# A two-stage kernel's 8th rows: from the absorb stage to sums over all modes at the end

## The chip, the core and the metric

The kernel runs on one core of a Trainium2 chip. The core has TensorE (PE in the profile; its weight loads are PEld), VectorE (DVE), ScalarE (ACT), GpSimd (POOL) and SyncE (SP), and 16 DMA engines that serve the transfers which SP and GpSimd issue. Each engine works through its own instructions in order. The metric is the device time of one execution in microseconds, as the median of several runs. The profile is of one execution more.

## The reference

Two stages in one kernel. The first is a linear attention over q, k, v of 8 batches, 8 heads, 576 rows and 64 columns; its result x has 8 batches of 576 rows and 512 columns. The second mixes x along the rows in the frequency domain and then along the columns:

```python
X = np.fft.rfft(x, axis=1)                     # 64 modes are kept
Yr = einsum('bmd,mde->bme', Xr, w_r) - einsum('bmd,mde->bme', Xi, w_i)
Yi = einsum('bmd,mde->bme', Xr, w_i) + einsum('bmd,mde->bme', Xi, w_r)
y = np.fft.irfft(Y, n=S, axis=1)               # Y is 0 beyond mode 63
u = x + y
return u + np.maximum(u @ w_ch, 0.0)
```

w_r and w_i are 64 matrices of 512 x 512 in f32, 134 MB together; every one is read once. w_ch is one matrix of 512 x 512.

## The kernel before

**Rows.** x lies in SBUF as bf16 (tile xs), in 36 chunks of 128 rows x 512 columns: (bp, n) with batch pair bp 0 to 3 and n 0 to 8. A batch's 576 rows are 64 groups of nine. Chunks n = 0 to 3 hold two of the first eight rows of the groups of the pair's first batch, n = 4 to 7 those of its second batch; chunk n = 8 holds the ninth row of the groups ("8th", counted from 0), of both batches, 64 partitions each. A matmul for n = 8 is therefore made in two halves of 64 output rows (`back`, line 681).

**Weights.** GpSimd issues the loads of the mode weights, cast to bf16 on the way: 64 tiles `wt` of 1 MB each, one for a quarter g of the columns and a group o of eight modes and the real or imaginary part. A load is issued when a buffer comes free, eight buffers in the pool `pw`. `mix` (line 447) multiplies a tile into the sums of its mode group, so TensorE takes each tile once, in the order of the loads.

**y and z.** When the last quarter of a mode group o is mixed (loop at line 848, g = 3, i = 1), the group's mode values are complete: yst (128 x 512). `put` (line 762) copies it to 16 partitions of 8 x 512, the rows from 16 o of `yall` for o under 6, and for o = 6 and 7 to `yl`, in two places of four (32 rows each). TensorE transposes yst and multiplies it by w_ch; that is zst, put to `zall` or to the other two places of `yl`. For o = 7 one of the two copies of each goes through GpSimd's queue, the other through SP's.

**Sums.** irfft is a matmul with a table of cosines and sines over the mode rows. CI is the table for the modes of o = 0 to 5 (96 rows), and it has rows for all 128; CL is the table for the rows of `yl` (o = 6, 7), CM that for o = 7 straight from yst. Since u @ w_ch = x @ w_ch + irfft(Y) @ w_ch, x and x @ w_ch (tile xw) are treated alike, y serves the one and z the other.

**Work that fills the waits for weights.** `todo` (line 753) is a list of steps, of which the loop takes a number after each mix, written in the line with `left`:

- `hold(i)`, one for each chunk: the chunk is transposed and multiplied by w_ch; ScalarE writes the product to xw. The last three chunks (i from K = 33) keep it in PSUM. It also advances the making of the tables (`inverse_tables`).
- the absorb steps (class Absorb, line 691): `all` adds the sums over the modes of o = 0 to 5 to a chunk: one matmul over `yall` for x, one with the identity for xw and one over `zall`; VectorE writes x back to xs, ScalarE xw. For the three held chunks there is only_x and only_w.

The number taken after each mix is such that A steps are left when seven mixes are left, and these are spread over the seven.

**The end.** `Last` (line 771) makes the output of two chunks (the first two and the last two of the list one by one): `base` puts xw or x into PSUM through a permutation or, for n = 8, the identity; `late` adds the sums over `yl`; `relu` is ScalarE's, from PSUM into the tile rl; `store` is VectorE's addition of PSUM and rl into a tile `of` or `ofr`, and SP's transfer to HBM. `seq` (line 844) is the order, with the pairs of n = 8 between those of the other chunks; the last loop (line 914) interleaves `base` and `late` of one entry with those of the next. PSUM has four single banks for the relu part (tag pt) and two pairs for the other (tag pp). Every instruction is kept in the order in which it is written.

Of the kernel before, what the change touches and what calls it, by code (L numbers as in the profile page):

```python
# [10 lines left out]
F32 = mybir.dt.float32  # L11
BF16 = mybir.dt.bfloat16
# [9 lines left out]
NP = 4  # L22
# [21 lines left out]
def kernel(  # L44
# [531 lines left out]
    yall = pw.tile([128, B_, DMODEL], BF16, name="yall", tag="wt")  # L576
    yl = pw.tile([128, B_, DMODEL], BF16, name="yl", tag="wt")
    CI = pb.tile([128, 5, 128], BF16, name="CI", bufs=1)
    CL = pb.tile([128, 5, 128], BF16, name="CL", bufs=1)
    perm = CF.rearrange("p c t x m -> p (c t x m)")[:, 512:640]  # L580
    dve.tensor_copy(perm.rearrange("k (p a) -> k a p", a=2),
                    ident_b.rearrange("k (a p) -> k a p", a=2))
# [3 lines left out]
    def inverse_tables():  # L586

        flat = xw[:, NP - 1].rearrange("p n e -> p (n e)").bitcast(F32)
        tok, ang, rnd = (flat[:, 640 * i:640 * i + 640] for i in range(3))
        small = pb.tile([128, 40], F32, name="small", bufs=1)  # L590
        ints = pb.tile([128, 16], I32, name="ints", bufs=1)
        for c in range(4):
            for a in range(2):
                dve.tensor_scalar_add(out=tok[:, 128 * c + 64 * a:128 * c + 64 * a + 64],
                                      in0=nine, scalar1=float(4 * a + c))
        for i in range(2):
            dve.tensor_scalar_add(out=tok[:, 512 + 64 * i:576 + 64 * i], in0=nine, scalar1=8.0)
        used = [0, 0]
        yield

        def bits(src, shift, mask):
            t, f = ints[:, used[0]:used[0] + 1], small[:, used[1]:used[1] + 1]
            used[0] += 1
            used[1] += 1
            dve.tensor_scalar(out=t, in0=src, scalar1=shift, scalar2=mask,
                              op0=ALU.logical_shift_right, op1=ALU.bitwise_and)
            dve.tensor_copy(f, t)
            return f

        def calc(in0, s1, s2, op0=ALU.mult, op1=ALU.add):  # L610
            f = small[:, used[1]:used[1] + 1]
            used[1] += 1
            dve.tensor_scalar(out=f, in0=in0, scalar1=s1, scalar2=s2, op0=op0, op1=op1)
            return f

        j, t, r = bits(pi, 2, 3), bits(pi, 1, 1), bits(pi, 0, 1)
        jt = calc(t, 4.0, j)
        mode = calc(bits(pi, 4, 7), 8.0, jt)
        late = calc(calc(bits(pi, 4, 1), 8.0, 48.0), 1.0, jt)
        jm, tm, rm, b0 = bits(pi, 5, 3), bits(pi, 4, 1), bits(pi, 3, 1), bits(pi, 0, 7)  # L620
        last = calc(calc(tm, 4.0, jm), 1.0, 56.0)
        b0 = calc(b0, 0.0, 1.0, ALU.is_equal, ALU.mult)
        yield
        for dst, m, r, only in ((CI, mode, r, None), (CL, late, r, None), (CM, last, rm, b0)):
            n = 512 if only is not None else 640
            ph = calc(r, -S_ / 4.0, S_ / 4.0)
            amp = calc(r, -4.0 / S_, 2.0 / S_)
            if m is mode:
                half = calc(calc(m, 0.0, -0.5, ALU.is_equal, ALU.mult), 1.0, 1.0)
                amp = calc(amp, half, 0.0)  # L630
            if only is not None:
                amp = calc(amp, only, 0.0)
            dve.tensor_scalar(out=ang[:, :n], in0=tok[:, :n], scalar1=m, scalar2=ph,
                              op0=ALU.mult, op1=ALU.add)
            dve.tensor_scalar(out=rnd[:, :n], in0=ang[:, :n], scalar1=1.0 / S_, scalar2=MAGIC,
                              op0=ALU.mult, op1=ALU.add)
            dve.tensor_scalar(out=rnd[:, :n], in0=rnd[:, :n], scalar1=-MAGIC,
                              scalar2=-float(S_), op0=ALU.add, op1=ALU.mult)
            dve.tensor_tensor(out=ang[:, :n], in0=ang[:, :n], in1=rnd[:, :n], op=ALU.add)
            yield  # L640
            act.activation(rnd[:, :n], ang[:, :n], ACT.Sin, scale=2.0 * math.pi / S_)
            if dst is CI:
                dve.tensor_scalar_mul(out=dst.rearrange("p c s -> p (c s)"), in0=rnd[:, :n],
                                      scalar1=amp)
                yield
                continue
            for c in range(4):
                dve.tensor_scalar_mul(
                    out=dst[:, c, :].rearrange("k (p a) -> k a p", a=2),
                    in0=rnd[:, 128 * c:128 * c + 128].rearrange("k (a p) -> k a p", a=2),  # L650
                    scalar1=amp)
            if dst is CL:
                dve.tensor_scalar_mul(out=dst[:, 4, :], in0=rnd[:, 512:640], scalar1=amp)
            yield

    class Channels:
# [73 lines left out]
            self.keep_w()  # L730

    chunks = [(bp, n) for bp in range(NP) for n in range(9)]
    ch = [Channels(*c) for c in chunks]
    ab = [Absorb(*c) for c in chunks]
    K = len(ch) - 3
# [15 lines left out]
        ch[i].hold(ab[i].q)  # L751

    todo = [ch[0].turn] + [lambda i=i: hold(i) for i in range(len(ch))]
    todo += [c.only_x for c in ab[K:]] + [c.only_w for c in ab[K:]] + [c.all for c in ab[:K]]
    A = 3 * 3 + K

    def fill(n):
        for _ in range(n):
            if todo:
                todo.pop(0)()  # L760

    def put(src, o, dst, copies):
        if o < 6:
            sp.dma_start(dst[16 * o:16 * o + 16], src)
        else:
            for s in copies:
                r = 32 * s + 16 * (o - 6)
                (sp, pool)[s // 2 if o == 7 else 0].dma_start(yl[r:r + 16], src)


    class Last:

        def __init__(self, *items):
            self.items = items
            bp, n = items[0]
            self.early = bp == 0 and n < 4
            self.first = bp == 0 and n < 2

        def base(self, which):
            if self.first:  # L780
                if which:
                    self.pp = banks()
                    self.q, self.p = [self.pp[:, 1]], [self.pp[:, 0]]
            elif which:
                self.q = [bank() for _ in self.items]
            else:
                self.pp = banks()
                self.p = [self.pp[:, a] for a in range(2)]
            for a, (bp, n) in enumerate(self.items):
                turned = perm if n < 8 else ident_b  # L790
                if which:
                    pe.matmul(self.q[a], lhsT=turned, rhs=xw[:, bp, n, :],
                              start=True, stop=False)
                else:
                    pe.matmul(self.p[a].rearrange("p (g e) -> p g e", g=4), lhsT=turned,
                              rhs=chunk(bp, n), start=True, stop=False)

        def late(self, which):
            for a, (bp, n) in enumerate(self.items):
                r = 64 * a + 32 * which  # L800
                back((self.q if which else self.p)[a], n, bp, CL, yl,
                     slice(r, r + 16 if self.early else r + 32), not self.early)
# [9 lines left out]
            act.copy(self.rl[:, 0], self.p[0])  # L812

        def relu(self):
            self.rl = pb.tile([128, 2, DMODEL], F32, name="rl")
            for a in range(len(self.items)):
                act.activation(self.rl[:, a], self.q[a], ACT.Relu)

        def store(self):
            (bp, n), w = self.items[0], len(self.items)  # L820
# [8 lines left out]
                dve.tensor_tensor(out=o, in0=self.p[0], in1=self.rl[:, 0], op=ALU.add)  # L829
            else:  # L830
                dve.tensor_tensor(out=o, in0=self.pp, in1=self.rl, op=ALU.add)
            if n == 8:
                sp.dma_start(
                    bass.AP(tensor=out.tensor, offset=out.offset + (2 * bp * S_ + 8) * DMODEL,
                            ap=[[9 * DMODEL, 128], [2 * S_ * DMODEL, 2], [1, DMODEL]]), o)
                return
# [4 lines left out]
                o.rearrange("p a e -> p (a e)") if w > 1 else o)  # L841

    pairs = [[((bp, n), (bp, n + 1)) for n in (0, 2, 4, 6)] for bp in range(NP)]
    seq = [Last((0, 0)), Last((0, 1))] + [Last(*x) for x in pairs[0][1:] + pairs[1]]
    seq += [Last((0, 8), (1, 8))] + [Last(*x) for x in pairs[2]] + [Last((2, 8), (3, 8))]
    seq += [Last(*x) for x in pairs[3][:3]] + [Last((3, 6)), Last((3, 7))]
    H = DMODEL // 2
    while mixq:
        key = mixq.pop(0)
# [13 lines left out]
        if g == NG - 1 and i == 1:  # L863
# [8 lines left out]
            for h in range(2):  # L872
                dve.tensor_tensor(out=yst[:, H * h:H * h + H], in0=py[:, H * h:H * h + H],
                                  in1=yacc[:, o, H * h:H * h + H], op=ALU.add)
            put(yst, o, yall, (0, 2))
            if o < 5:
                fill(min(n, 1))
            for h in range(2):
# [22 lines left out]
            act.copy(zst[:, 0:H], pz[0])  # L901
            dve.tensor_copy(zst[:, H:], pz[1])
            put(zst, o, zall, (1, 3))
            fill(max(n - 2, 0) if o < 5 else n)
        else:
            fill(n)
# [7 lines left out]
    for g, s in enumerate(seq):  # L914
# [12 lines left out]
        if t:  # L927
            t.straight(1)
            t.relu()
        s.store()  # L930
    pb_cm.__exit__(None, None, None)
    pw_cm.__exit__(None, None, None)

# [28 lines left out]
```

## Time and profile before

| | |
|---|---|
| median of 7 runs | 444.36 us (443.9 to 445.51) |
| profiled execution, its own time | 444.95 us |
| its span, first to last instruction | 443.1 us |
| TensorE busy, with weight loads beside it | 343.1 us (77%), 218.6 us (49%) |
| VectorE, ScalarE, GpSimd busy | 284.3 (64%), 279.7 (63%), 84.5 us (19%) |
| DMA moved | 99.31 MB, mean 224 GB/s |
| HBM read, written | 163.64 MB, 9.44 MB |
| chain that ended last, largest shares | issue 32%, PE 26%, DMA 15%, ACT 10% |

The span is cut into 40 slices of 11 us. A digit of a slice is the busy share in tenths. A group of instructions is named by its engine, operation and tiles, `out<-in`, with the shape. Line numbers in the profile are those of a helper (L37) for all, so the tiles tell what an instruction is. Times of an instruction are from the start of the span. A transfer lands when all 16 of its parts have. The chain of waits is followed back from the last instruction, at each step to what released it.

### The profile page before, as it was taken

How to read it: one execution, taken by the hardware profiler on the slowest of the kernel's cores; microseconds unless marked ns; L12 is line 12 of the kernel's file. 1: busy time of each engine (PE TensorE's matmuls, PEld its weight loads, DVE VectorE, ACT ScalarE, POOL GpSimd, SP SyncE). 2: the span in 40 equal slices, each digit the busy share in tenths (PEclk: the TensorE clock that was granted, in tenths of full speed). 3: DMA queues.
4: the chain of work that ended last, by engine and by line, in shares of the span. 5: the costliest groups of instructions: out<-in, count | busy, mean ns of one | idle time of the engine just before them, and what ended most of it. 6: DMA issues, size and time to landing. Idle time of an engine off the chain costs nothing.

```text
span 443.1 us, 10508 instructions
## 1 busy us (share of the span) xinstructions
PE 343.1 (77%) x4433; PEld 218.6 (49%) x4433; DVE 284.3 (64%) x561; ACT 279.7 (63%) x488; POOL 84.5 (19%) x126
## 2 busy tenths in 40 slices
PE   3577669677687685885976877886899779999994
PEld 2355547545465573664754655653455434343231
DVE  4657585555765757867668568658834223776685
ACT  4588697666977967867778659433444222665673
POOL 7132122122211212321232121141012110000000
PEclk9979897689988969988889789698999888999998
DMA  8999999999999999999999999999999999993697
GB/s 168 236 211 210 238 211 237 238 212 264 210 213 237 238 236 235 212 238 211 239 222 227 236 213 238 212 212 212 212 224 221 219 219 219 211 221 69 215 383 286
DMA packets 51487, 99.31 MB, mean 224 GB/s; under 512 B 2480, under 2 KB 13616, under 8 KB 51440
## 3 DMA queue, kind: packets, MB, share of 16 engines
q0 software_dynamic: 45280, 86.19, 99.0%
q1 hardware_dynamic: 6160, 12.45, 8.0%
q8 instruction: 34, 0.56, 0.5%
q14 instruction: 13, 0.11, 0.1%
HBM read 163.64 MB, written 9.44 MB: 391 GB/s over the span
## 4 chain that ended last, share of the span: by engine, by line
issue 32%; PE 26%; DMA 15%; ACT 10%; DVE 8%; POOL 7%; POOLq 0%; ACTq 0%; DVEq 0%
DMA wt<-in_moe_w_i_dram 13%; PE pt L37 8%; PE one L37 7%; PE pp L37 5%; PE two L37 5%; POOL wt L37 4%; ACT AB L37 4%; DVE m L37 3%; DVE mk L37 2%; ACT AQ L37 2%; DMA qb<-in_q_dram 1%; ACT XT L37 1%; POOL kb L37 1%; POOL qb L37 1%; POOL vn L37 1%
## 5 line engine op out<-in xcount | busy, mean ns | idle before, releaser
L37 ACT ACTIVATE AB<-two 128x1024 bf16<-128x1024 f32 x64 | 62.1, 1028 | 12.1 <-DVE mk L37 8.6
L37 ACT ACTIVATE AQ<-two 128x1024 bf16<-128x1024 f32 x64 | 62.7, 1047 | 3.5 <-PE two L37 3.4
L37 ACT CAST xw<-pt 128x512 bf16<-128x512 f32 x50 | 29.4, 587 | 40.5 <-PE pt L37 34.9
L37 DVE TENSOR_REDUCE mk<-two 128x8 f32<-128x1024 f32 x32 | 38.9, 1219 | 14.7 <-PE two L37 14.7
L37 DVE TENSOR_REDUCE m<-two 128x8 f32<-128x1024 f32 x32 | 39.2, 1224 | 12.7 <-PE two L37 12.5
L37 DVE RECIPROCAL rd<-one 128x6 f32<-128x6 f32 x48 | 9.4, 196 | 56.0 <-PE one L37 55.9
L37 PE MATMUL pt<-wchb,xT 128*128 128x512 bf16 x136 | 38.2, 407 | 5.8 <-DVE xT L37 4.7
L37 DVE TENSOR_TENSOR va<-vn,ee 128x1152 bf16<-128x1152 f32 x32 | 42.0, 1355 | 0.0
L37 ACT COPY kT<-one 128x512 bf16<-128x512 bf16 (+1 forms) x32 | 19.3, 640 | 31.0 <-PE one L37 30.8
L37 PEld LDWEIGHTS <-xs 128*128 128x128 bf16 x624 | 32.3, 104 | 12.9 <-issue 7.1
L37 PEld LDWEIGHTS <-minus 96*128 96x128 bf16 x288 | 27.9, 115 | 17.5 <-issue 12.3
L37 PE MATMUL two<-w2blk,qT 128*128 128x256 bf16 x128 | 20.8, 289 | 19.1 <-ACT AB L37 9.2
L37 POOL DMA_DIRECT2D wt<-in_moe_w_r_dram x30 | 22.3, 744 | 69.2 <-PE one L37 34.8
L37 POOL DMA_DIRECT2D wt<-in_moe_w_i_dram x28 | 20.9, 746 | 72.6 <-PE one L37 40.0
L37 PE MATMUL two<-qT,w2blk 128*128 128x512 bf16 x64 | 30.2, 472 | 3.8 <-ACT AQ L37 3.7
L37 PEld LDWEIGHTS <-qT 128*128 128x128 bf16 x144 | 14.3, 102 | 36.7 <-issue 33.9
L37 PE MATMUL one<-wt,XT 128*32 128x512 bf16 x304 | 26.6, 436 | 6.1 <-DVE XT L37 2.7
L37 PE MATMUL two<-mT,minus 96*128 96x128 bf16 x256 | 30.7, 255 | 0.0
L37 PE MATMUL one<-kvz,AQ 128*128 128x65 bf16 x512 | 29.5, 217 | 0.0
L37 DVE TENSOR_TENSOR xs<-one,rd 128x384 bf16<-128x384 f32 x48 | 26.8, 557 | 1.6
L37 PEld LDWEIGHTS <-XT 128*32 128x32 bf16 x512 | 14.4, 149 | 26.1 <-issue 14.5
L37 PE MATMUL two<-w2blk,kT 128*128 128x256 bf16 x128 | 21.2, 294 | 7.9 <-ACT AB L37 7.9
(131 smaller groups left out, 701.0 us busy)
## 6 DMA issues: line engine op xcount, KB each, us to landing
wt<-in_moe_w_r_dram POOLq DMA_DIRECT2D x30, 1024.0 KB, 22.2
wt<-in_moe_w_i_dram POOLq DMA_DIRECT2D x28, 1024.0 KB, 22.0
vn<-in_v_dram POOLq DMA_DIRECT2D x15, 576.0 KB, 17.9
out_dram<-of SPq DMA_DIRECT2D x16, 512.0 KB, 3.1
kb<-in_k_dram POOLq DMA_DIRECT2D x16, 288.0 KB, 15.5
qb<-in_q_dram POOLq DMA_DIRECT2D x16, 288.0 KB, 15.5
xs<-in_moe_w_i_dram POOLq DMA_DIRECT2D x2, 1024.0 KB, 24.5
yacc<-in_moe_w_r_dram POOLq DMA_DIRECT2D x1, 1024.0 KB, 9.5
```

What stands on the lines that cost most here:

```text
L37: ins = f(*args, **kwargs)
```

## The change

The four chunks n = 8 are no longer absorbed. They come first in the list of chunks, and the three chunks that are held in PSUM are now (3,5), (3,6) and (3,7) instead of (3,6), (3,7) and (3,8). At the end their sums run over all 128 rows of `yall` and `zall` with the table CI, in one matmul per half; for this the rows of o = 6 and 7 are put into `yall` and `zall` as well, by one more copy on SP after each put (list `rest`). `base` for x is dropped; GpSimd adds x to the relu's output in place (tile rx, from the pool `pw`), and VectorE adds the sum from PSUM as before. The two entries of n = 8 leave `seq`; their first half is done at the end of the last loop's steps 3 and 9, their second half and store at the end of steps 5 and 11. CL loses its fifth column block.

```diff
--- before.py
+++ after.py
@@ -576,7 +576,8 @@
     yall = pw.tile([128, B_, DMODEL], BF16, name="yall", tag="wt")
     yl = pw.tile([128, B_, DMODEL], BF16, name="yl", tag="wt")
     CI = pb.tile([128, 5, 128], BF16, name="CI", bufs=1)
-    CL = pb.tile([128, 5, 128], BF16, name="CL", bufs=1)
+    CL = pb.tile([128, 4, 128], BF16, name="CL", bufs=1)
+    rest = []
     perm = CF.rearrange("p c t x m -> p (c t x m)")[:, 512:640]
     dve.tensor_copy(perm.rearrange("k (p a) -> k a p", a=2),
                     ident_b.rearrange("k (a p) -> k a p", a=2))
@@ -622,7 +623,7 @@
         b0 = calc(b0, 0.0, 1.0, ALU.is_equal, ALU.mult)
         yield
         for dst, m, r, only in ((CI, mode, r, None), (CL, late, r, None), (CM, last, rm, b0)):
-            n = 512 if only is not None else 640
+            n = 640 if dst is CI else 512
             ph = calc(r, -S_ / 4.0, S_ / 4.0)
             amp = calc(r, -4.0 / S_, 2.0 / S_)
             if m is mode:
@@ -649,8 +650,6 @@
                     out=dst[:, c, :].rearrange("k (p a) -> k a p", a=2),
                     in0=rnd[:, 128 * c:128 * c + 128].rearrange("k (a p) -> k a p", a=2),
                     scalar1=amp)
-            if dst is CL:
-                dve.tensor_scalar_mul(out=dst[:, 4, :], in0=rnd[:, 512:640], scalar1=amp)
             yield
 
     class Channels:
@@ -730,6 +729,7 @@
             self.keep_w()
 
     chunks = [(bp, n) for bp in range(NP) for n in range(9)]
+    chunks.sort(key=lambda c: c[1] < 8)
     ch = [Channels(*c) for c in chunks]
     ab = [Absorb(*c) for c in chunks]
     K = len(ch) - 3
@@ -751,8 +751,8 @@
         ch[i].hold(ab[i].q)
 
     todo = [ch[0].turn] + [lambda i=i: hold(i) for i in range(len(ch))]
-    todo += [c.only_x for c in ab[K:]] + [c.only_w for c in ab[K:]] + [c.all for c in ab[:K]]
-    A = 3 * 3 + K
+    todo += [c.only_x for c in ab[K:]] + [c.only_w for c in ab[K:]] + [c.all for c in ab[NP:K]]
+    A = 3 * 3 + K - NP
 
     def fill(n):
         for _ in range(n):
@@ -763,6 +763,7 @@
         if o < 6:
             sp.dma_start(dst[16 * o:16 * o + 16], src)
         else:
+            rest.append((dst[16 * o:16 * o + 16], src))
             for s in copies:
                 r = 32 * s + 16 * (o - 6)
                 (sp, pool)[s // 2 if o == 7 else 0].dma_start(yl[r:r + 16], src)
@@ -775,6 +776,7 @@
             bp, n = items[0]
             self.early = bp == 0 and n < 4
             self.first = bp == 0 and n < 2
+            self.direct = n == 8
 
         def base(self, which):
             if self.first:
@@ -787,7 +789,9 @@
                 self.pp = banks()
                 self.p = [self.pp[:, a] for a in range(2)]
             for a, (bp, n) in enumerate(self.items):
-                turned = perm if n < 8 else ident_b
+                turned = ident_b if self.direct else perm
+                if self.direct and not which:
+                    continue
                 if which:
                     pe.matmul(self.q[a], lhsT=turned, rhs=xw[:, bp, n, :],
                               start=True, stop=False)
@@ -797,6 +801,10 @@
 
         def late(self, which):
             for a, (bp, n) in enumerate(self.items):
+                if self.direct:
+                    back((self.q if which else self.p)[a], n, bp, CI, zall if which else yall,
+                         slice(0, 128))
+                    continue
                 r = 64 * a + 32 * which
                 back((self.q if which else self.p)[a], n, bp, CL, yl,
                      slice(r, r + 16 if self.early else r + 32), not self.early)
@@ -812,9 +820,16 @@
             act.copy(self.rl[:, 0], self.p[0])
 
         def relu(self):
-            self.rl = pb.tile([128, 2, DMODEL], F32, name="rl")
+            if self.direct:
+                self.rl = pw.tile([128, 2, DMODEL], F32, name="rx", tag="wt")
+            else:
+                self.rl = pb.tile([128, 2, DMODEL], F32, name="rl")
             for a in range(len(self.items)):
                 act.activation(self.rl[:, a], self.q[a], ACT.Relu)
+            if self.direct:
+                for a, c in enumerate(self.items):
+                    x = self.rl[:, a].rearrange("p (g e) -> p g e", g=4)
+                    pool.tensor_tensor(out=x, in0=x, in1=chunk(*c), op=ALU.add)
 
         def store(self):
             (bp, n), w = self.items[0], len(self.items)
@@ -829,7 +844,7 @@
                 dve.tensor_tensor(out=o, in0=self.p[0], in1=self.rl[:, 0], op=ALU.add)
             else:
                 dve.tensor_tensor(out=o, in0=self.pp, in1=self.rl, op=ALU.add)
-            if n == 8:
+            if self.direct:
                 sp.dma_start(
                     bass.AP(tensor=out.tensor, offset=out.offset + (2 * bp * S_ + 8) * DMODEL,
                             ap=[[9 * DMODEL, 128], [2 * S_ * DMODEL, 2], [1, DMODEL]]), o)
@@ -841,9 +856,9 @@
                 o.rearrange("p a e -> p (a e)") if w > 1 else o)
 
     pairs = [[((bp, n), (bp, n + 1)) for n in (0, 2, 4, 6)] for bp in range(NP)]
-    seq = [Last((0, 0)), Last((0, 1))] + [Last(*x) for x in pairs[0][1:] + pairs[1]]
-    seq += [Last((0, 8), (1, 8))] + [Last(*x) for x in pairs[2]] + [Last((2, 8), (3, 8))]
+    seq = [Last((0, 0)), Last((0, 1))] + [Last(*x) for x in pairs[0][1:] + pairs[1] + pairs[2]]
     seq += [Last(*x) for x in pairs[3][:3]] + [Last((3, 6)), Last((3, 7))]
+    whole = {5: Last((0, 8), (1, 8)), 11: Last((2, 8), (3, 8))}
     H = DMODEL // 2
     while mixq:
         key = mixq.pop(0)
@@ -873,6 +888,8 @@
                 dve.tensor_tensor(out=yst[:, H * h:H * h + H], in0=py[:, H * h:H * h + H],
                                   in1=yacc[:, o, H * h:H * h + H], op=ALU.add)
             put(yst, o, yall, (0, 2))
+            if rest:
+                sp.dma_start(*rest.pop())
             if o < 5:
                 fill(min(n, 1))
             for h in range(2):
@@ -901,6 +918,8 @@
             act.copy(zst[:, 0:H], pz[0])
             dve.tensor_copy(zst[:, H:], pz[1])
             put(zst, o, zall, (1, 3))
+            if rest:
+                sp.dma_start(*rest.pop())
             fill(max(n - 2, 0) if o < 5 else n)
         else:
             fill(n)
@@ -928,6 +947,16 @@
             t.straight(1)
             t.relu()
         s.store()
+        if g + 2 in whole:
+            d = whole[g + 2]
+            d.base(1)
+            d.late(1)
+            d.relu()
+        if g in whole:
+            d = whole[g]
+            d.base(0)
+            d.late(0)
+            d.store()
     pb_cm.__exit__(None, None, None)
     pw_cm.__exit__(None, None, None)
```

## The prediction

> **What bounds the kernel now.** I read the slices of the page, then the chain of waits, then the weight loads one by one, because the change takes TensorE work out of the last 45 us and adds transfers there. The page's DMA line comes first.
>
> ```profile
> DMA  8999999999999999999999999999999999993697
> q0 software_dynamic: 45280, 86.19, 99.0%
> ```
>
> The 16 DMA engines are full in every slice but the last four: the weights are the bound until shortly before the end. The chain of waits (start, length, what) shows the last wait on weights and the end:
>
> ```profile
> 329.47 31.97 DMA wt<-in_moe_w_i_dram
> ...
> 406.26 0.60 PE pt L37 x7
> ...
> 410.43 3.68 DMA yl<-zst
> ...
> 437.37 0.69 DVE ofr L37
> ```
>
> From 361.5 the chain names TensorE (PE) alone, so 4 us less of it looks like 4 us gained. The view by tile of the last load and of the copies at mode group 6, and the timeline of the mixes that take the last loads, say otherwise:
>
> ```profile
> L37 POOL DMA_DIRECT2D wt<-in_moe_w_i_dram x1: 740/740/740, 370.2 to 370.2; - x1
> DMA to landing us min/median/max: 35.2/35.2/35.2
> ```
>
> ```profile
> L37 SPq DMA_DIRECT2D yl<-yst x2: 547/570/592, 386.7 to 387.3; - x2
> L37 SPq DMA_DIRECT2D yl<-zst x2: 547/574/602, 388.8 to 389.4; - x2
> DMA to landing us min/median/max: 6.6/9.4/10.4
> ```
>
> ```profile
> 402.05 0.66 PE L37 MATMUL pt<-wt,XT 128*32 128x512 bf16 x8
> ...
> 406.19 0.67 PE L37 MATMUL pt<-wt,XT 128*32 128x512 bf16 x8
> ```
>
> The last weight lands at 370.2 + 35.2 = 405.4 and its mix starts at 406.19: 0.8 us of slack. Asked the same way, the loads issued at 342.1, 346.5, 351.9, 357.3 and 362.9 took 35.3, 35.9, 35.7, 36.1 and 37.5: they land at 377.4, 382.4, 387.5, 393.4 and 400.4, against mixes at 379.4, 385.1, 392.4, 397.0 and 402.05. TensorE is never far behind the stream. Two stretches of the clock matter too (length, busy time of PE, PEld, DVE, ACT, POOL, clock, DMA share, GB/s):
>
> ```profile
> 357.95:361.36 3.41, 1.32 (x10) 0.65 (x8) 0.42 (x1) 1.17 (x2) 0.10 (x1) 1.00 1.12 216
> 361.36:364.77 3.41, 2.56 (x16) 1.05 (x16) 1.05 (x3) 0.37 (x1) 0.74 (x1) 0.50 1.12 218
> ```
>
> TensorE was busy 39% of one stretch and ran at half clock in the next.
>
> **What the skill says.** "DMA: Bandwidth & Descriptors", on queues, rings and completion order: an engine goes round between the queues that have work, packet by packet. The trace agrees: a copy from SP lands in 3.4 us at 407.7, when nothing else moves, and in 6.6 to 10.4 us at 387, inside the stream; each takes the stream's time. "TensorE: Matmul & The Clock Gate", Part 1: a free-running window of about 3.4 us with little work halves the clock of the next. The stretches above agree. "GPSIMD Engine Reference", section 3.1: a two-input add of 2048 f32 columns takes 4497 ns; no GpSimd add is in this trace. Its section 1 has GpSimd contend with VectorE instructions that have two SBUF inputs; the tail's VectorE adds read one operand from PSUM, so I expect none.
>
> **The change, part by part.**
>
> *Absorb stage, removed.* Four `all` steps go. A step of an 8th row takes 1.00 us of PE (five matmuls, 398.99 to 399.99), another 0.655 (three at 0.218). The three held chunks become (3,5) to (3,7), so the removed ones are three of the first kind and one of the second, and the two half-width pairs of (3,8) (0.33) become single passes (0.22): 3.0 + 0.655 + 0.22 = 3.9 us of PE. VectorE loses four adds of 0.69 and ScalarE four casts of 0.59, both beside PE. By the quotas of the filling rule all four go before the second last mix. The shorter CL table and the other order of the holds lie before 361.5, where PE waited 2.2 us for weights; without that cover they are some tenths.
>
> *Copies, added.* SP issues four more copies of 128 KB, each behind the put of its y or z. Two fall into the stream (group 6). The spacing of landings without copies is 5.0 and 5.1 (377.4, 382.4, 387.5); the next three took 17.9 in place of 15.1 with four copies among them, so 0.7 per copy, and two more cost 1.4: the last load lands at 406.8, the one before at 401.8 (the copies come earlier, since PE is ahead). Bounds: 0, if the slowest DMA engine had other work, and 2 x 1.0. I take 1.4, since all engines share each copy.
>
> *What then bounds the last mix.* PE is at the second last mix at 402.05 - 3.9 = 398.2 and waits until 401.8. A wait of 3.6 us leaves one clock window mostly idle, so the next 3.41 us run at half clock and lose up to 1.7. What lies between the last two mixes takes 4.14 (402.05 to 406.19): PE is ready at 405.9, or 407.6 in the bad case. With the load at 406.8 I take 407.2: **+1.0 us** (from -0.8, copies free, to +1.5). The 3.9 us become idle time.
>
> *Behind the last mix.* The chain y, transposes, z, put, landing (7.96 us to 414.15) stays. The third y copy on SP is out at 408.8, before SP's z put at 409.89. The third z copy (410.45) shares the engines with GpSimd's z put (410.43), which releases the tail at 414.11: eight packets more per engine against it, and so does the first store's in the kernel before; **+0.3** (0 to 0.7). SP's queue then holds the first store, wanted at 411.13 and free to go at 411.0.
>
> *The tail.* A usual step of two rows is 1.30 us of PE (415.75 to 417.05), 1.24 of VectorE and 512 KB, which at 400 GB/s is 1.31: three engines equally full. Each of the two 8th-row items made two steps 1.63 long: 2 x 1.63 - 1.30 = 1.96, together 3.92. Now each item puts 2 base passes (0.44) and two half-width pairs (0.22 each and 0.1 for the switch) in one place, where nothing is stored, and the next base waits about 0.1 for a bank that ScalarE reads late: 1.1 us without a store. Two steps later come two pairs and a store, 0.54 on PE but 1.24 on VectorE, which now sets the pace. VectorE: 2 x (1.1 + 1.24) = 4.7; it regains 0.06 per step over some six steps: 4.35. At 1.31 per store DMA regains less: **+0.6** in all. Bounds: -0.7 (PE alone: 2 x (0.44 + 0.54 + 0.1 + 0.54) - 3.92), +0.9.
>
> GpSimd: 512 / 2048 of 4497 ns is 1.12 us, say 1.2 with its start, two per item, hidden by the two steps until the item's store. By the same step times they may take 1.6 each; beyond that VectorE waits in order, with all later stores behind it: each 0.1 more costs 0.4 (two adds, two items). From below: a free add gains nothing.
>
> *Sum.* 1.0 + 0.3 + 0.6 = 1.9. The profiled execution took 444.95 (its span of 443.1 and 1.85 around it) and would take 446.85; it is 0.59 over the median of the runs, so **446.3 us** for the median, 0.4% slower. I take any difference under 0.2% (0.9 us) as none.
>
> **The rivals.** (1) The stream doesn't mind the copies and PE counts: the last mix starts at 405.45 (-0.75), the put is not disturbed, the tail gains its 0.7 of PE: 442.9, faster; were PE the only bound, 3.9 + 0.7 less, 439.8. For it: the chain of waits names PE. Against: the landing at 405.4. It decides from copies under 0.27 each (2 x 0.27 - 0.75 - 0.7 = -0.9). (2) A draw: copies at 0.35 each with the clock kept up (+0.3 at the mix), +0.1 at the put, +0.3 in the tail: 445.0. (3) GpSimd is late: 2.2 us per add, 0.6 over its cover, 4 x 0.6 = 2.4 more: 448.7. (4) The new copies write rows 96 to 127 of tiles of which absorb reads rows 0 to 95; if the waits went by tile, PE would stand for a copy at group 6 (6.6 to 10.4, partly in its new slack). Against: matmuls read yl at 409.24 while a copy into its next 16 rows is under way. It would add some 4: 450.
>
> **Chances.** Forecast 0.62, (1) 0.12, (2) 0.16, (3) 0.07, (4) 0.03. The forecast's own range is 445.3 to 447.4 (its terms at +0.6, 0, +0.3 and at +1.4, +0.7, +0.9). The range for 8 in 10 leaves out (3), (4) and about half of (1): 443.8 to 447.8. Slower: 0.70 (the forecast, (3), (4), less a little that falls under 0.2%); faster 0.12; the same 0.18.
>
> **What would show it.** Right: PE idle about 3 us before the second last mix, behind a weight; the last weight landing 1 to 1.5 later than 405.4; some 3.4 us at half clock near 403; six SP copies in a row at group 6; in the tail two gaps of about 2.4 between stores, VectorE without gaps after them. Wrong: the last landing at 405.4; no idle PE before 406; VectorE waiting for GpSimd; ten or more us between a copy's issue and the next absorb matmul.

## The result, and the profile after

The changed kernel takes 448.84 us (median of 12 runs, 447.2 to 451.32); the kernel before, on the same chips, 445.04 (31 runs). The ratio is 1.0092, 95% interval 1.0078 to 1.0107: 4.1 us slower, where 1.9 us slower was predicted. (The ratio is over all runs, close to that of the means; the two medians lie 3.8 us apart.) The profiled execution took 451.32 us with a span of 449.5; it is the longest of the twelve, so its losses are on the large side.

The page of the changed kernel, its line of the DMA engines' busy tenths and that of SP's queue, which had 6160 packets and 12.45 MB before:

```profile
DMA  8999999999999999999999999999999999995498
q1 hardware_dynamic: 6736, 12.98, 9.2%
```

The engines are full as long as before; the slices between the stream and the stores have 5 and 4 where they had 3 and 6. The timeline of the last two mixes after (start, length; in brackets the idle time before it and what ended it), and the last load's landing by tile:

```profile
402.06 0.66 PE L37 MATMUL pt<-wt,XT 128*32 128x512 bf16 x8 [2.73 <-DMA wt<-in_moe_w_r_dram]
...
407.56 0.66 PE L37 MATMUL pt<-wt,XT 128*32 128x512 bf16 x8
```

```profile
L37 POOL DMA_DIRECT2D wt<-in_moe_w_i_dram x1: 740/740/740, 370.9 to 370.9; - x1
...
DMA to landing us min/median/max: 35.8/35.8/35.8
```

TensorE's saved work has become a wait of 2.73 us for a weight, and the last mix starts at 407.56 instead of 406.19, 0.9 us behind the landing at 406.7. That 0.9 is the clock: from one mix to the next TensorE took 5.50 us, where it took 4.14 before. The stretches of the clock's grid after (length, busy PE, PEld, DVE, ACT, POOL, clock, DMA share, GB/s):

```profile
399.59:403.00 3.41, 0.94 (x10) 0.42 (x10) 0.39 (x1) 0.90 (x2) 0.00 (x0) 1.00 1.07 179
403.00:406.41 3.41, 3.41 (x10) 1.06 (x7) 1.29 (x2) 1.14 (x2) 0.00 (x0) 0.50 0.42 79
...
413.24:416.65 3.41, 1.89 (x9) 0.49 (x7) 1.52 (x2) 0.96 (x3) 0.00 (x0) 1.00 1.15 116
416.65:420.06 3.41, 2.63 (x9) 0.54 (x8) 0.00 (x0) 0.94 (x2) 0.00 (x0) 0.50 0.81 291
420.06:423.48 3.42, 3.42 (x13) 0.74 (x10) 1.22 (x1) 2.17 (x4) 0.79 (x1) 0.50 0.14 56
```

There are two stretches at half clock. The first, from 403.00, I had predicted. The second lasts 6.8 us, stands at the start of the tail and was in no step of mine. What leads to it is in the chain of waits after, and in the timelines of the first matmuls that read the two z puts, after and then before:

```profile
411.81 5.58 DMA yl<-zst
417.39 0.04 issue
417.43 1.55 PE pt L37 x3
...
443.83 0.69 DVE ofr L37
```

```profile
415.98 0.37 PE L37 MATMUL pt<-yl,CL 32*128 32x512 bf16 x1 [1.22 <-DMA yl<-zst]
...
417.43 0.58 PE L37 MATMUL pt<-yl,CL 32*128 32x512 bf16 x1 [1.08 <-DMA yl<-zst]
```

```profile
414.15 0.37 PE L37 MATMUL pt<-yl,CL 32*128 32x512 bf16 x1 [0.43 <-DMA yl<-zst]
```

GpSimd's put of z, which releases the tail, took 5.58 us from issue to landing in place of 3.68. TensorE stood 1.22 us for SP's put and 1.08 for GpSimd's, where it had stood 0.43. The span's 6.4 us (449.5 - 443.1) fall apart at these marks: last mix 407.56 against 406.19, +1.4; last mix to landing of the z put 9.83 against 7.92, +1.9; landing to the start of the last VectorE addition 26.44 against 23.26, +3.2.

### The profile page after: what moved, and what is told of

Same layout as the page of the kernel before. It is cut to its first block, busy times and chain, and to the rows that moved or that the text cites. A ratio compares the mean times of both kernels' runs of the same rounds, so it can differ in the third digit from the quotient of the medians.

```text
span 449.5 us, 10464 instructions
## 1 busy us (share of the span) xinstructions
PE 344.9 (77%) x4409; PEld 219.5 (49%) x4409; DVE 281.1 (63%) x556; ACT 278.0 (62%) x484; POOL 89.0 (20%) x130
## 5 line engine op out<-in xcount | busy, mean ns | idle before, releaser
L37 ACT CAST xw<-pt 128x512 bf16<-128x512 f32 x48 | 28.2, 587 | 37.6 <-PE pt L37 33.9
L37 PE MATMUL pt<-wchb,xT 128*128 128x512 bf16 x136 | 37.1, 397 | 6.9 <-DVE xT L37 5.6
L37 PE MATMUL one<-kvz,AQ 128*128 128x65 bf16 x512 | 31.1, 223 | 0.0
L37 POOL DMA_DIRECT2D kb<-in_k_dram x16 | 11.5, 718 | 88.8 <-PE one L37 87.2
L37 PEld LDWEIGHTS <-AQ 128*128 128x128 bf16 x512 | 27.9, 119 | 1.6 <-issue 0.4
```

The source lines that it names most:

```text
L37: ins = f(*args, **kwargs)
```

## The experiments

All ratios are to the kernel before, run on the same chip; microseconds are what the ratio makes of 444.9, so they can differ by some tenths from the difference of two medians. "Behind the last mix" means the two copies of mode group 7, "in the stream" those of group 6.

**Each part alone.** First the four copies alone, in the kernel before:

```diff
         else:
+            rest.append((dst[16 * o:16 * o + 16], src))
             for s in copies:
...
             put(yst, o, yall, (0, 2))
+            if rest:
+                sp.dma_start(*rest.pop())
...
             put(zst, o, zall, (1, 3))
+            if rest:
+                sp.dma_start(*rest.pop())
```

> The kernel before with nothing but the four new copies on SP (into rows of yall and zall that nothing reads); all 8th rows are absorbed as before. Theory A (the copies are the cost: two in the weight stream hold the last load back by about 1.3 us, two behind the last mix hold the z put back by about 2 us): the last mix about 0.5 us later than before, the z put's landing about 2 us later, 447.0 to 448.5. Theory B (the tail with its GpSimd adds and gaps is the cost): 445.0 to 445.5.

It took 448.17 us, ratio 1.0078 (1.0057 to 1.0100), +3.5 us. The copies by themselves make nearly the whole loss. The last load landed at 406.3, 44.9 us after the eighth load before it (43.9 before); GpSimd's z put took 5.56.

The 8th rows not absorbed, alone:

```diff
+    chunks.sort(key=lambda c: c[1] < 8)
...
-    todo += [c.only_x for c in ab[K:]] + [c.only_w for c in ab[K:]] + [c.all for c in ab[:K]]
-    A = 3 * 3 + K
+    todo += [c.only_x for c in ab[K:]] + [c.only_w for c in ab[K:]] + [c.all for c in ab[NP:K]]
+    A = 3 * 3 + K - NP
```

> The kernel before with the chunks of the 8th rows put first and not absorbed, nothing else: no new copies, the old tail. It leaves the modes of groups 0 to 5 out of the 8th rows. Theory A: TensorE's 3.9 us become a wait for weights, the last mix starts at 405.4 to 406.2, 444.2 to 445.0. Rival (the new wait before the second last mix halves the clock and costs more than it gives): 445.5 or more.

It took 443.69 us, ratio 0.9987 (0.9977 to 0.9998), -0.6 us. That is half a microsecond under theory A's range, but the kernel before took 444.41 on this chip. 3.9 us of TensorE work are worth 0.6. The timeline of the mixes:

```profile
395.11 0.66 PE L37 MATMUL pt<-wt,XT 128*32 128x512 bf16 x8
400.23 0.66 PE L37 MATMUL pt<-wt,XT 128*32 128x512 bf16 x8 [1.07 <-DMA wt<-in_moe_w_r_dram]
405.24 0.66 PE L37 MATMUL pt<-wt,XT 128*32 128x512 bf16 x8 [0.81 <-DMA wt<-in_moe_w_i_dram]
```

TensorE waits for the last two loads, and its last mix starts 0.04 us after the landing at 405.20.

The changed tail alone; the diff is to the changed kernel:

```diff
-    chunks.sort(key=lambda c: c[1] < 8)
...
-    todo += [c.only_x for c in ab[K:]] + [c.only_w for c in ab[K:]] + [c.all for c in ab[NP:K]]
-    A = 3 * 3 + K - NP
+    todo += [c.only_x for c in ab[K:]] + [c.only_w for c in ab[K:]] + [c.all for c in ab[:K]]
+    A = 3 * 3 + K
...
-            if rest:
-                sp.dma_start(*rest.pop())
...
-            if rest:
-                sp.dma_start(*rest.pop())
...
-                     slice(0, 128))
+                     slice(0, 96))
```

> The changed tail alone: 8th rows absorbed as before, no new copies, the tail of the changed kernel with the sums over 96 rows (so it counts groups 0 to 5 twice for the 8th rows and leaves 6 and 7 out). My term of +0.6 us: 445.3 to 446.0. Theory B (the tail is the cost): 447 or more. GpSimd's two adds 2.3 us per item, hidden.

It took 445.30 us, ratio 1.0015 (1.0003 to 1.0027), +0.7 us. VectorE's and GpSimd's timelines of this kernel:

```profile
419.23 2.52 DVE L37 TENSOR_TENSOR of<-pp,rl 128x1024 f32<-128x1024 f32 x2 [1.14 <-PE pp L37]
421.67 1.21 DVE L37 TENSOR_TENSOR of<-pp,rx 128x1024 f32<-128x1024 f32 x1
422.89 5.11 DVE L37 TENSOR_TENSOR of<-pp,rl 128x1024 f32<-128x1024 f32 x4
```

```profile
418.43 2.27 POOL L37 TENSOR_TENSOR rx<-rx,xs 128x512 f32<-128x512 f32 x2 [6.54 <-issue]
```

There is one gap ahead of the item (1.14 us, while TensorE makes the sums of its relu part); then VectorE goes without a gap through the item (rx) and behind it. GpSimd's two adds end at 420.70, 1.0 us before VectorE reads rx.

**Which copies.** The two in the stream and the two behind the last mix, each pair alone in the kernel before; the diff, to the kernel with all four copies and at both places, is of group 6 alone, and with `o == 7` it is group 7 alone:

```diff
-            if rest:
+            if rest and o < 7:
                 sp.dma_start(*rest.pop())
```

> The kernel before with the two new copies of group 6 alone, inside the weight stream. If they cost the stream 0.3 to 0.7 us each, the last load lands 0.6 to 1.4 us later, of which 0.8 is slack: 444.4 to 445.2. If half of the cost of the four copies is theirs: 446 or more.

> The kernel before with the two new copies of group 7 alone, behind the last mix. Theory A, now with its size from the run with all four copies: the z put on GpSimd's queue takes 5.6 us in place of 3.7, and TensorE's wait for it brings a stretch at half clock in some phases: 447.3 to 448.5, nearly all of the loss. Rival (the four add up evenly): 446.2.

Group 6 alone took 445.36 us, ratio 1.0010 (0.9998 to 1.0021), +0.4, just over the expected range. Group 7 alone took 448.48 us, ratio 1.0074 (1.0049 to 1.0099), +3.3. So the loss is behind the last mix. The view by tile of the z put on GpSimd's queue, group 7 alone:

```profile
L37 POOL DMA_DIRECT2D yl<-zst x1: 544/544/544, 409.6 to 409.6; - x1
...
DMA to landing us min/median/max: 5.6/5.6/5.6
```

**What of it: bytes and order, or the 16 partitions.** The same two copies, into 128 partitions:

```diff
+    dump = pb.tile([128, 2, DMODEL], BF16, name="dump", bufs=1)
...
-            rest.append((dst[16 * o:16 * o + 16], src))
+            rest.append((dump[:, 0 if dst is yall else 1], src))
```

> The same two copies of group 7, as many bytes in packets of the same 1 KB from the same tiles, but each into 128 partitions of a tile that nothing reads, not into 16. If the queue's order or the bytes delay the z put, it stays at 5.6 us and the time at 447 to 448.5. If it is the landing in 16 partitions, the packets of 1 KB stay near 50 ns behind one another, not 175, the z put takes 3.7 to 4.3, and the time is 444.4 to 445.3.

It took 445.38 us, ratio 1.0005 (0.9994 to 1.0016), +0.2, at the upper end of the second range. The same put:

```profile
L37 POOL DMA_DIRECT2D yl<-zst x1: 544/544/544, 409.3 to 409.3; - x1
...
DMA to landing us min/median/max: 4.2/4.2/4.2
```

With the same bytes and the same place in the queue the put is 0.5 us late instead of 1.9, and 3.1 of the 3.3 us go. So most of the cost lies in where the copies land, and only 0.5 us is left for their bytes and their order. Two things changed together, though. The narrow copies go into 16 partitions, and these are 112 to 127, the ones that GpSimd's z put goes to as well. Sharing them is not needed for a delay: SP's z put goes to partitions 48 to 63, and with the narrow copies it landed 1.2 us later too (4.65 us against 3.42). Whether it makes the rest of GpSimd's 1.9 was not tried.

One part of the expectation failed. A packet of 1 KB took 56 ns in the mean for a copy with nothing before it and 176 for the narrow copies behind it (about 200 packets in 2 us, some 100 GB/s); with the wide copies it still took 141 for about a microsecond. So following closely on another copy slows packets either way; narrow ones keep them slow for much longer (from 410.5 to 415 in the run with all four). GpSimd's own y put, into partitions 80 to 95, is under way at the same time in both, so the part of each isn't separated. Where in the DMA path packets queue was not tried.

**How much of it is the clock.** Zero-weight matmuls (`zw` is a tile of zeros) that keep TensorE busy in the wait, in `late` of the kernel with group 7's copies; `warm` is 4 for `t.late(1)` in step 2 and 0 elsewhere:

```diff
+                for _ in range(warm):
+                    pe.matmul(self.q[a], lhsT=zw, rhs=xw[:, bp, n, :], start=False, stop=False)
                 r = 64 * a + 32 * which
```

> The kernel with the two copies of group 7 alone, and eight matmuls with zero weights where TensorE waits for the two z puts (four before each of the two first sums over them, 0.9 us each, inside waits of 1.2 and 1.1 us), which add zero. If the stretch at half clock that follows the wait is the larger part of the 3.3 us, it goes and the time falls to 446.0 to 446.9 (only the 1.9 us of the late put stay). If the late put alone is the cost: 448 to 448.5.

It took 446.73 us, ratio 1.0049 (1.0032 to 1.0065), +2.2, inside the range of the first theory. The stretches around the put, of the kernel with group 7's copies and then of the one with the extra matmuls (the second pair is not on the clock's grid, but at full clock throughout):

```profile
411.09:414.51 3.42, 1.82 (x8) 0.48 (x7) 1.45 (x2) 1.01 (x3) 0.00 (x0) 1.00 1.14 115
414.51:417.92 3.41, 2.75 (x9) 0.54 (x8) 0.00 (x0) 0.81 (x2) 0.00 (x0) 0.50 0.81 294
```

```profile
412.00:415.40 3.40, 3.14 (x16) 1.13 (x15) 1.72 (x2) 1.41 (x3) 0.00 (x0) 1.00 1.11 111
415.40:418.80 3.40, 3.25 (x16) 1.00 (x16) 0.25 (x2) 1.41 (x3) 0.00 (x0) 1.00 1.06 294
```

The half clock is gone, while the put took 5.53 as before. From its landing to the last addition it is 23.26 us, as in the kernel before, against 26.04. So 1.9 us are the late put and the rest is the clock. By the ratios the clock is about 1.1 of the 3.3, though the two intervals overlap; where it happens the profiles show 1.6 (all four copies) and 2.8 (group 7's alone). The single runs fit a clock that falls in some executions and not in others: of the eleven with group 7's copies, three took 445.5 to 446.0 us and eight 448.2 to 450.3, with none between. The eight runs with the extra matmuls took 446.2 to 448.1. Only the profiled runs show where the clock fell, so this reading of the two groups is likely, not shown.

**The changed kernel with its copies elsewhere.** Group 7's behind the first two stores; the diff is to the changed kernel, its first part at both places:

```diff
-            if rest:
+            if rest and o < 7:
                 sp.dma_start(*rest.pop())
...
-    whole = {5: Last((0, 8), (1, 8)), 11: Last((2, 8), (3, 8))}
+    whole = {7: Last((0, 8), (1, 8)), 13: Last((2, 8), (3, 8))}
...
         s.store()
+        if g == 1:
+            for c in rest[1::2] + rest[::2]:
+                sp.dma_start(*c)
```

> The changed kernel with the two new copies of group 7 moved on SP's queue behind the first two stores, and the two 8th-row items two steps later (7 and 13 in place of 5 and 11), so that they don't wait for those copies. Theory A: the z put lands 3.7 us after its issue again, no second stretch at half clock, 445.5 to 446.8. Theory B: as the changed kernel, 448.5 to 449.

It took 445.85 us, ratio 1.0030 (1.0017 to 1.0043), +1.3; the z put took 3.65 us and no half clock followed. Then all four there (the lines with `if rest:` taken out):

> The changed kernel with all four new copies on SP behind the first two stores, and the 8th-row items at steps 7 and 13. The last load lands at 405.4 or before, the last mix starts right behind it (0.7 us before that of the kernel before), the z put takes 3.7; the tail's own cost of 0.7 to 0.9 stays and the four copies share the engines with the first stores: 444.2 to 445.3, no gain on the kernel before. If the 8th-row items have to wait for the copies: 446.

It took 444.76 us, ratio 0.9997 (0.9988 to 1.0007), the time of the kernel before. The last load landed at 404.93 and the mix started at 404.97. Behind it this profile has 3.4 us at half clock (405.99 to 409.40). The next edit keeps TensorE busier ahead of the last mix:

```diff
             seq[0].late(0)
+            for _ in range(3):
+                pe.matmul(seq[0].q[0], lhsT=zw, rhs=xw[:, 0, 0, :], start=False, stop=False)
         mix(*key, wts.pop(key), XTb[g % 2], bank)
```

> The kernel with all four copies late, and three matmuls with zero weights (0.65 us) in its wait of 0.8 us before the last mix, which add zero. If the stretch at half clock behind the last mix (y's transposes and z's product at double length, about 1.5 us) comes from that wait, it goes: 443.3 to 444.2. If not: 444.5 to 445.

It took 444.13 us, ratio 0.9987 (0.9979 to 0.9996), and its profile has no half clock behind the last mix. The interval overlaps that of the version without; whether the three matmuls gain anything stays open.

**A version below both.** The weight stream is what the last mix waits for, so this version takes copies out of it: all four new copies are late, and two of group 6's old puts are held.

```diff
             for s in copies:
                 r = 32 * s + 16 * (o - 6)
+                if o == 6 and s > 1:
+                    held6.append((yl[r:r + 16], src))
+                    continue
...
             assert not todo
+            for c in held6:
+                act.dma_start(*c)
             seq[0].base(1)
```

> The changed kernel with all four new copies behind the first two stores, 8th-row items at steps 7 and 13, and the two puts of group 6 into yl's places 2 and 3, which nothing needs before step 2, issued on ScalarE's queue just before the last mix. The weight stream has two copies in place of four: the last load lands 0.6 to 1.3 us earlier (403.7 to 404.8), the last mix right behind it, 2 us before that of the kernel before. With the tail's 0.7 to 0.9: 443.2 to 444.2, the first version below the kernel before. If the two held puts collide with y's of group 7 or the clock falls: 444.5 to 446.

It took 443.00 us (442.75 to 443.39), ratio 0.9964 (0.9950 to 0.9978), 1.6 us faster than the kernel before and a little better than expected. None of the 32 runs of the kernel before beside it was under 443.52. Its last mixes:

```profile
398.77 0.66 PE L37 MATMUL pt<-wt,XT 128*32 128x512 bf16 x8 [0.73 <-DMA wt<-in_moe_w_r_dram]
403.67 0.66 PE L37 MATMUL pt<-wt,XT 128*32 128x512 bf16 x8 [0.70 <-DMA wt<-in_moe_w_i_dram]
```

The held puts alone, in the kernel before, tell whether the smaller TensorE work has a part in it:

> The kernel before with the two puts of group 6 held for ScalarE's queue just before the last mix, and nothing else: 8th rows absorbed, old tail. If both are needed for a gain (a shorter weight stream and less TensorE work ahead of the last mix), the last mix stays at TensorE's own 406.2 though the last load lands near 404, and the time is the kernel before's: 444.3 to 445.2. If the held puts alone made the gain: 442.9 to 443.5.

It took 445.35 us, ratio 1.0011 (1.0000 to 1.0021), no gain. Its load issued at 368.9 took 34.9 and landed at 403.8, but

```profile
400.80 0.66 PE L37 MATMUL pt<-wt,XT 128*32 128x512 bf16 x8
404.93 0.66 PE L37 MATMUL pt<-wt,XT 128*32 128x512 bf16 x8
```

show TensorE without a wait: its own work now holds the mix, 1.2 us behind the landing, and the mixes are 4.13 us apart as before (4.14). A part of the missing gain is lost elsewhere: the z put took 4.17 us here, and landed 8.41 us after the last mix where it had been 7.92. Stream and TensorE were 0.8 us apart, so taking from either alone gains little, and taking from both gains.

## Why the prediction was wrong

The direction was right, and so was the mechanism of three of the four terms. The fourth, the put behind the last mix, was mis-sized, and what follows from a late put was missing; so the sum was half of what came. By its steps:

- *Copies in the stream, 0.7 each.* Right over the profiles together. From the landing of the eighth load before the last to the last load, kernels with two narrow copies in group 6 took 42.0 and 42.4 us, eight kernels with four 42.6 to 43.9 (mean 43.1), four with six 44.3 to 44.9 (mean 44.6): 0.5 to 0.8 per copy. At the 219 GB/s of these slices 128 KB would take 0.60. The last load landed at 406.7, predicted 406.8; part of that agreement is luck, since this profile's stream was already 0.7 late at 362, and from there its two copies more cost 0.6 together, not 1.4.
- *TensorE's 3.9 us become idle time; half clock before the last mix; together +1.0.* Right in this profile: a wait of 2.73 (predicted 3.6), the clock halved from 403.00 to 406.41, the last mix at 407.56 (predicted 407.2). The size is less sure. By the ratios the removal alone gave -0.6 and the copies of group 6 +0.4; the version with both, the new tail and group 7's copies late gave +1.3, which leaves 0.6 for these two steps. In that version's profile the wait was 2.23 us and no half clock followed (below), so the clock's part depends on where the wait falls.
- *The tail, +0.6.* Right: +0.7 alone, and 0.45 from the z landing to the last addition in its profile. GpSimd's adds took 2.27 us per item (predicted 2.4) and were covered; that is 1.13 per add, against 1.12 estimated from the figure in section 3.1 of the Trainium skill's "GPSIMD Engine Reference". VectorE's additions beside them took 1.22 as elsewhere, so no contention showed. My rival (3) fell.
- *The put behind the last mix, +0.3 (0 to 0.7).* This is the step that failed: the put landed 1.9 us later, in each of the four profiles with those copies there (5.53 to 5.58 against 3.68). I counted eight packets more per engine; at the 56 ns of a copy that has the engines to itself they are 0.45 us. But the y copy before it had not drained: SP's third y copy took 5.2 us to land, and SP's z put, queued behind it, 4.7 in place of 3.4. I had asked when SP was free to issue, 408.8, not when the transfer was over. The views by tile of the two in the changed kernel:

```profile
L37 SPq DMA_DIRECT2D yall<-yst x1: 598/598/598, 409.6 to 409.6; - x1
...
DMA to landing us min/median/max: 5.2/5.2/5.2
```

```profile
L37 SPq DMA_DIRECT2D yl<-zst x1: 547/547/547, 411.3 to 411.3; - x1
...
DMA to landing us min/median/max: 4.7/4.7/4.7
```

- *What follows from a late put.* Missing altogether. I used the clock's rule for the wait that I had found and not for the wait that a late put makes. The kernel before waited 0.43 us there, which hid that any 2 us more could leave a clock window half idle. By the ratios this is worth about 1.1 us.

Two readings behind the prediction were too narrow. I counted one window of 3.41 us at half clock, but the kernel before was at half clock from 361.36 to 368.19, two windows. And Part 1 of "TensorE: Matmul & The Clock Gate" in the Trainium skill speaks of an idle window; the stretch that I showed was busy 39%, so "little work" is what this trace shows, not the page's words.

The parts alone sum to -0.6 + 0.4 + 3.3 + 0.7 = +3.8, against 4.1 measured. Their intervals are too wide to show or to exclude that two of them together cost some tenths more than each alone. Rival (4) fell too: absorb matmuls ran on while the copies of group 6 were under way.

## What to carry to other kernels

Before removing work from an engine, look up when the transfer that its last step needs lands: 0.8 us of slack was the most that 3.9 us could give, until the stream itself was made shorter. A small copy added between two critical ones is not free because its queue is idle at issue; ask when the copies ahead of it will have landed, above all when they go to few partitions. And each new wait of TensorE has to be asked a second time, for the clock that follows it.

## What the runs showed of the hardware

- A copy of 128 KB into 16 partitions, alone, moves its 1 KB packets in 56 ns in the mean; with another narrow one right before it they take 176, and a put queued behind lands 1.2 to 1.9 us later. Into 128 partitions the same extra copies delayed it by 0.5.
- The stretch ahead of a half-clock one was busy with matmuls for 28%, 53% and 55% of its time in the lines shown, but 72% in the version with all copies late (402.58 to 405.99). In the version that only leaves out the absorbing, a stretch with nearly the same work, busy 72% too (402.65 to 406.06), was followed by full clock. So busy time alone does not decide there; what else counts was not tried. In the version with group 7's copies late, a stretch busy for 51% was followed by full clock:

```profile
399.67:403.08 3.41, 1.73 (x13) 0.80 (x14) 0.38 (x2) 0.56 (x2) 0.00 (x0) 1.00 0.80 126
403.08:406.50 3.42, 2.59 (x17) 0.92 (x15) 1.65 (x3) 1.66 (x3) 0.00 (x0) 1.00 0.25 47
```

- On each profile's own grid, in all 14 profiles from 340 to 436 us, the 17 full-clock stretches with TensorE busy under 40% were all followed by half clock, and of seven between 51% and 59% two were. Of the stretches at half clock, the 11 busy up to 81% were followed by another at half clock, and the 20 busy 94% or more were not. The 6.8 us of the second one in the changed kernel fit this: its first half held the end of the wait and was busy 77%.
